# Fourier mixing followed by routed experts: x loaded in larger transfers, and the first stage of the third and fourth batch moved to other places in the head

## The chip, the cores and the metric

The kernel runs on one core of a Trainium2 chip. A core has TensorE (PE, matrix products; PEld in the profile is its loading of weights), VectorE (DVE), ScalarE (ACT), GpSimd (POOL) and SyncE (SP, which here only issues transfers). SP, ACT and POOL each have a queue of DMA transfers; 16 DMA engines move the data of all of them. The metric is the device time of one execution in microseconds (us). Durations in the profile come from one profiled execution.

## The reference

```python
X = np.fft.rfft(x, axis=1)                 # x: 8 batches x 2496 x 256, float32
Y = X * (filt_r + 1j * filt_i)[None]
y = np.fft.irfft(Y, n=2496, axis=1)        # then seen as 19968 rows of 256
expert_idx = token_ids * 2654435761 % 8
for e in range(8):
    h = np.maximum(y[expert_idx == e] @ w1[e], 0)    # w1[e]: 256 x 1024
    out[expert_idx == e] = h @ w2[e]                 # w2[e]: 1024 x 256
```

Each of the eight batches is filtered along its 2496 positions, and each resulting row then goes through the two layers of one of eight experts, chosen by its token's number.

## The kernel before

**Fourier part.** 2496 = 39 x 64. Positions of a batch are read as 39 x 64, and three of the 64 columns are put side by side, so that a product has 3 x 39 = 117 rows. A batch goes through four products. Stage 1 (`stage1`, tiles `pa`, line 267) transforms along 39 with the table `wf_t`; it is cut into six pieces `u`, two for each of three x parts `v`; the sixth piece is small (line 261). The forward product (`pb`, line 312) transforms along 64; VectorE multiplies with the filter (lines 318 and 322) and adds (line 323), which gives `y`. The back product (`pc`, lines 335 and 378) goes back along 64, and the inverse product (`pd`, line 267 in `stage3`) back along 39. Between stage 1 and the forward product, and between the back and the inverse product, rows and columns have to be exchanged. From the third batch on this goes through DRAM (`d1`, `d2`: written at lines 297, 342, 792 and 794, read by `load2`, line 303, into `low`, and by `load4`). For the first batch, and for the way back of the second, TensorE transposes (`pt` line 367, `pu` line 394). The results `o` are scattered to `xs` in DRAM, sorted by expert (line 433, on GpSimd's queue, four issues for a piece).

**Experts.** `xs` is cut into tiles of 256 rows. `step(i)` gathers a tile (`load`, `xg`, line 843), transposes it on VectorE (`xt`, line 854), forms sums of its halves (`st`, line 867) and of the weights (`tw`, line 876: GpSimd, for tile 0 VectorE), multiplies up (`up`, line 886, banks `up_a`, `up_b`, `up_c`), adds on VectorE (line 893), applies the ReLU on ACT (line 890), and multiplies down (`dps`, line 921). `ask` issues the gathers of a tile some steps ahead.

**Order.** Every engine has one program order. It comes from a list of pieces with due times. The head (`head`, lines 763 to 796) holds the first batch, the second, the third's stage 1 and four of six pieces of the fourth's stage 1, and ends with the gathers of tiles 0 and 1. All after it is `main`, whose pieces have due times in steps: `run_until` issues those that are due between the parts of an expert step. A piece's instructions go on all its engines at that place of the order, its transfers among them. The fourth batch is `batches[3]`, the third `batches[2]`; `first` and `second` are batches 0 and 1.

**Buffers.** The PSUM pool `fps` has four buffers in rotation, shared by `pa`, `pb`, `pc` and `pd`. `pa` is copied out by ACT. `high` holds the second batch's back products first, and then the fourth's stage 1 in two slots `t1`, so that the third x part's results go where the first part's were. x parts of the third and fourth batch use the pool `xpool` of two buffers. `put_off` collects writes to `d1` that are issued on SP after the first gathers. The loads of x (`load1`, line 249) are three transfers of 39 rows to a part, one for each third of the columns; one of the first batch's is on ACT's queue and all others are on SP's. Eight semaphores serve the transfers of SP and ACT in turn, so an issue waits for the transfer that used its semaphore last.

The numbers of lines are those of the kernel before; the changed kernel's are up to three higher behind line 290.

## Time and profile before

| | us |
|---|---|
| median of 6 runs | 1426.33 |
| lowest, highest | 1419.26, 1428.30 |
| profiled execution, whole | 1424.15 |
| its span in the profile | 1422.4 |
| TensorE busy in it | 1376.1 |
| last scatter of the second batch issued | 139.80 |
| first expert step's first product | 146.47 |
| second expert step's first product | 164.81 |

The span begins with the first instruction and ends with the last. A row of the timeline gives start, length, engine, line, operation, what it writes and reads, how many instructions stand together, and in brackets the idle time of the engine before it and who ended it. The chain of waits is followed back from the last instruction: each row's engine or transfer was what the next row waited for. The granted clock is the share of TensorE's full clock that it was given; over the whole span it was 0.988.

### The profile page before, as it was taken

The page shows a single profiled execution, that of the slowest core. Times are in us where ns is not written, and L with a number is a line of the kernel's source. Part 1 is how long each engine was busy: PE and PEld are TensorE (multiplying, and loading weights), DVE is VectorE, ACT ScalarE, POOL GpSimd, SP SyncE. Part 2 cuts the span into 40 slices and gives each one's busy share as a digit, 9 for nine tenths or more (in the row PEclk, how much of TensorE's full clock was granted, in tenths as well). Part 3 has the DMA queues.
Part 4 walks back from the last instruction along what each step waited for, and adds up shares of the span by engine and source line. Part 5 has one row for each costly group of instructions (what it writes and reads, how often), then busy time and mean ns, then how long its engine had stood idle before and what let it go on. Part 6 is the DMA issues. An engine that isn't in the chain of part 4 may idle for free.

```text
span 1422.4 us, 26307 instructions
## 1 busy us (share of the span) xinstructions
PE 1376.1 (97%) x9398; PEld 1276.4 (90%) x9398; DVE 888.2 (62%) x1630; ACT 417.3 (29%) x760; POOL 829.5 (58%) x735
## 2 busy tenths in 40 slices
PE   7989888999999999999999999999999999999997
PEld 7777777998888888889999899999999999999997
DVE  6673475575556466445666477656767776676775
ACT  3554122232223223232223222222222222222222
POOL 5166332854574565578533687788855566555563
PEclk8999999999999999999999999999999999999999
DMA  8685865767987598888754775887742526161611
GB/s 223 185 293 165 211 199 139 229 202 246 275 266 252 156 292 275 259 273 277 245 166 120 234 255 170 235 239 238 255 135 68 190 64 197 46 218 42 215 46 35
DMA packets 244650, 278.34 MB, mean 196 GB/s; under 512 B 125171, under 2 KB 213862, under 8 KB 235092
## 3 DMA queue, kind: packets, MB, share of 16 engines
q1 hardware_dynamic: 98020, 182.34, 40.9%
q10 hardware_dynamic: 126688, 50.07, 14.7%
q0 software_dynamic: 19808, 44.20, 8.8%
q8 instruction: 77, 1.26, 0.4%
q14 instruction: 57, 0.47, 0.1%
HBM read 293.65 MB, written 86.15 MB: 267 GB/s over the span
## 4 chain that ended last, share of the span: by engine, by line
PE 85%; DMA 8%; DVE 4%; issue 1%; ACT 1%; SPq 1%; ACTq 0%; POOLq 0%; POOL 0%; DVEq 0%
PE dps L921 20%; PE up_b L886 8%; PE up_a L886 5%; PE up_c L886 5%; PE pd L267 5%; PE pb L312 4%; PE dnc L948 4%; PE pa L267 4%; PE dnb L948 4%; PE dna L948 4%; PE upc L943 4%; PE upa L943 4%; PE pc L335 3%; DMA t<-d 2%; PE upe L943 2%; PE upb L943 2%
## 5 line engine op out<-in xcount | busy, mean ns | idle before, releaser
L921 PE MATMUL dps<-wts,ht 128*128 128x256 f32 x1600 | 367.0, 380 | 4.3 <-ACT ht L890 4.3
L921 PEld LDWEIGHTS dps<-wts,ht 128*128 128x128 f32 x1600 | 302.1, 190 | 47.7 <-ACT ht L890 5.5
L1013 POOL DMA_INDIRECT out_dram<-osb,no x158 | 164.4, 1040 | 222.8 <-DVE osb L955 137.3
L433 POOL DMA_INDIRECT xs<-o,sidx x176 | 178.4, 1014 | 167.4 <-ACT o L269 95.7
L876 POOL TENSOR_TENSOR tw<-wts 128x512 f32<-128x512 f32 x158 | 205.1, 1298 | 113.0 <-DMA wts<-in_moe_w_dram 88.7
L876 POOL TENSOR_TENSOR tw<-wts,tw 128x512 f32<-128x512 f32 x158 | 206.7, 1308 | 6.2
L893 DVE TENSOR_TENSOR ht<-up_b,ht 128x512 f32<-128x512 f32 x150 | 103.7, 692 | 113.6 <-PE up_b L886 91.3
L890 ACT ACTIVATE ht<-ht 128x512 f32<-128x512 f32 x150 | 94.3, 630 | 188.2 <-DVE ht L893 172.5
L322 DVE TENSOR_TENSOR z<-pb,filt 64x512 f32<-64x512 f32 x160 | 110.1, 688 | 30.8 <-PE pc L335 28.8
L926 DVE COPY osb<-dps 128x512 f32<-128x512 f32 x50 | 34.6, 691 | 148.1 <-PE dps L921 147.7
L886 PE MATMUL up_a<-xt,wts 128*128 128x128 f32 x800 | 115.7, 278 | 6.4 <-DVE xt L854 4.0
L886 PEld LDWEIGHTS up_a<-xt,wts 128*128 128x128 f32 x800 | 106.3, 194 | 10.0 <-DVE xt L854 4.4
L886 PE MATMUL up_b<-st,tw 128*128 128x128 f32 x800 | 107.4, 278 | 2.7 <-DVE ht L893 1.9
L886 PEld LDWEIGHTS up_b<-st,tw 128*128 128x128 f32 x800 | 98.2, 193 | 4.6 <-issue 4.6
L893 DVE TENSOR_TENSOR ht<-up_c,ht 128x512 f32<-128x512 f32 x100 | 69.1, 691 | 38.1 <-PE up_c L886 33.4
L952 ACT ACTIVATE ht<-ht 128x512 f32<-128x512 f32 x90 | 56.5, 630 | 122.5 <-DVE ht L955 76.6
L267 PE MATMUL pd<-t,wi_t 120*117 120x256 f32 x320 | 79.7, 393 | 2.9 <-DMA t<-d 2.3
L318 DVE TENSOR_TENSOR y<-pb,filt 128x512 f32<-128x512 f32 x80 | 55.2, 690 | 42.8 <-PE pb L312 40.6
L269 ACT COPY o<-pd 117x512 f32<-117x512 f32 x80 | 45.0, 585 | 102.1 <-PE pd L267 46.7
L267 PEld LDWEIGHTS pd<-t,wi_t 120*117 120x117 f32 x320 | 59.2, 189 | 15.6 <-DMA t<-d 3.0
L323 DVE TENSOR_TENSOR y<-y,z 128x512 f32<-128x512 f32 x80 | 71.1, 889 | 2.7
L312 PE MATMUL pb<-low,d_t 128*128 128x256 f32 x280 | 72.2, 381 | 0.0
(215 smaller groups left out, 2407.7 us busy)
## 6 DMA issues: line engine op xcount, KB each, us to landing
wts<-in_moe_w_dram SPq DMA_DIRECT2D x162, 1024.0 KB
xg<-xs ACTq DMA_DIRECT2D x321, 64.0 KB
low<-d SPq DMA_DIRECT2D x70, 256.0 KB
d_t<-t2s SPq DMA_DIRECT2D x15, 1024.0 KB
e_t<-t2s SPq DMA_DIRECT2D x15, 1024.0 KB
x<-in_x_dram SPq DMA_DIRECT2D x39, 312.0 KB
t<-d SPq DMA_DIRECT2D x12, 960.0 KB
raw<-in_moe_w_dram SPq DMA_DIRECT2D x8, 1024.0 KB
```

The source lines that it names most:

```text
L267: nc.tensor.matmul(out=ps[0:cols * H, k, :], lhsT=w[:], rhs=src[:, 2 * i + k, :], start=True, stop=True)
L312: nc.tensor.matmul(out=ps[:, i, :], lhsT=d_t[:, s, :], rhs=rhs, start=True, stop=True)
L322: nc.vector.tensor_tensor(out=z[b], in0=ps[a], in1=f_t[1][64 * hi:64 * hi + 64, s1:s1 + 2, :], op=OP.mult)
L433: st = nc.gpsimd.indirect_dma_start(out=xs[:], out_offset=bass.IndirectOffsetOnAxis(ap=index, axis=0), in_=rows, in_offset=None, bounds_ch ...
L876: eng.tensor_tensor(t[k][:], p, q, op=OP.subtract)
L886: nc.tensor.matmul(out=ps[bank][:, f, :], lhsT=w[:, f * P:(f + 1) * P], rhs=xx, start=first and f == 0, stop=True, skip_group_check=True)
L890: nc.scalar.activation(out=out, in_=in_, func=AF.Relu)
L893: nc.vector.tensor_tensor(out, ps[bank][:], other, op=OP.add)
L921: nc.tensor.matmul(out=ps[:, h, :], lhsT=ht[:, h, fp, :], rhs=w2[:, fp, :], start=(fp == 0), stop=(fp == FP - 1))
L943: nc.tensor.matmul(out=ps[:, f, :], lhsT=w[:, f * P:(f + 1) * P], rhs=xx, start=first and f == 0, stop=True, skip_group_check=True)
L948: nc.tensor.matmul(out=ps[:, 0, :], lhsT=a[:, f, :], rhs=b[:, f, :], start=first and f == 0, stop=True, skip_group_check=True)
L1013: st = nc.gpsimd.indirect_dma_start(out=out[:], out_offset=bass.IndirectOffsetOnAxis(ap=to_rows[i][:, h:h + 1], axis=0), in_=o[:, h, :], i ...
```

## The change

1. x is loaded in one transfer to a part, of 117 rows, all on SP's queue; the first part of the first batch in two transfers of four columns each. For this the rows of x and of the table `wf` stand in another order.
2. The third's stage 1 has other due times: its pieces 0 and 1 come before the second's last two back products, its piece 5 before the second's last inverse products, and no longer behind all of them.
3. All six pieces of the fourth's stage 1 are in the head, behind the second's inverse products. VectorE copies them out, not ACT. The write of x part 0's results to `d1` is issued at once on SP; those of parts 1 and 2 are put off. The last x part is loaded between pieces 1 and 2, into the buffer of the first.
4. In steps 0 and 1 the gathers of a later tile are asked for behind `up` and not inside it.

```diff
-        wf[:, h, h] = w
+        wf[:, H0[h] // HN, h] = w
...
-            for h in range(H):
-
-                (nc.scalar if self.b == 0 and h == 1 else nc.sync).dma_start(out=xt[h:NR:H, 0:n, :],
-                                  in_=bass.AP(tensor=x.tensor, offset=x.offset + (self.b * S + H0[h] + XL * v) * C,
-                                              ap=[[N2 * C, N1], [C, n], [1, C]]))
+            for j in (range(0, n, XG) if self.b == 0 and v == 0 else (0,)):
+                m = XG if self.b == 0 and v == 0 else n
+                nc.sync.dma_start(out=xt[:, j:j + m, :],
+                                  in_=bass.AP(tensor=x.tensor, offset=x.offset + (self.b * S + XL * v + j) * C,
+                                              ap=[[N2 * C, N1], [HN * C, H], [1, m * C]]))
...
-            self.products(wf_t, (NR, NR), 2 * NS, self.x[v][:, sl, :], self.t1[:, sl, :], nc.scalar.copy, u, "pa")
+            self.products(wf_t, (NR, NR), 2 * NS, self.x[v][:, sl, :], self.t1[:, sl, :],
+                          nc.vector.tensor_copy if self.b == 3 else nc.scalar.copy, u, "pa")
...
-                if (self.b == 2 and v > 0) or (self.b == 3 and v < 2):
+                if (self.b == 2 or self.b == 3) and v > 0:
...
-                    (nc.sync if self.b == 1 else nc.scalar).dma_start(out=dram, in_=chip)
+                    (nc.sync if self.b in (1, 3) else nc.scalar).dma_start(out=dram, in_=chip)
...
-    head += [(93.3 + 4.6 * u + 4 * (u > 3), lambda u=u: third.stage1(u)) for u in range(NU)]
+    head += [(t, lambda u=u: third.stage1(u)) for u, t in enumerate((87, 89.9, 93, 97.5, 107, 107.1))]
...
-    head += [(t, lambda v=v: fourth.load1(v)) for v, t in enumerate((110.5, 110.6))]
+    head += [(t, lambda v=v: fourth.load1(v)) for v, t in enumerate((95, 99, 118.025))]
...
-    head += [(123 + .1 * u, lambda u=u: fourth.stage1(u)) for u in range(4)]
+    head += [(t, lambda u=u: fourth.stage1(u)) for u, t in enumerate((118.01, 118.02, 118.03, 118.04, 118.1, 118.2))]
...
-    todo += part3(2, spaced(4.6, 7.5, NU), [4.0, 4.1, 4.8]) + part1(3, [None] * 4 + [1.5, 2], [None, None, .5])
+    todo += part3(2, spaced(4.6, 7.5, NU), [4.0, 4.1, 4.8])
...
-        up(i, ht, lambda: ask(i))
+        up(i, ht, (lambda: ask(i)) if i > 1 else (lambda: None))
+        if i < 2:
+            ask(i)
```

## The prediction

> **What bounds the kernel now.** I read the page first, then the windows of 10 us, then the chain of waits over the first 220 us, then the order in time around the gaps, and SyncE's queue.

> ```profile
> span 1422.4 us, 26307 instructions
> ...
> PE 1376.1 (97%) x9398; PEld 1276.4 (90%) x9398; DVE 888.2 (62%) x1630; ACT 417.3 (29%) x760; POOL 829.5 (58%) x735
> ...
> PEclk8999999999999999999999999999999999999999
> ```

> TensorE is busy for 97% of the span, so only its idle or half-clocked time can be won, and all but a few us of that lies before 200 us: after that a stage costs what its products cost, and a lead or a lag gained before it stays to the end. The digits of PEclk are all 9 but the first; two of the windows say where the rest of the clock goes (columns: stretch, length, busy us of PE, PEld, DVE, ACT, POOL, granted clock, DMA share, GB/s).

> ```profile
> 100.00:110.00 10.00, 6.22 (x29) 4.88 (x28) 5.59 (x9) 1.54 (x3) 1.86 (x2) 0.73 0.79 279
> ...
> 140.00:150.00 10.00, 6.04 (x28) 5.34 (x27) 2.48 (x5) 2.89 (x5) 5.67 (x5) 0.78 0.62 125
> ```

> TensorE is idle for 3.8 and 4.0 us there and the granted clock is 0.73 and 0.78. The chain of waits names what is behind it (start, us, what):

> ```profile
> 3.94 10.49 DMA wts<-in_x_dram
> ...
> 14.53 8.04 PE pa L357 x56
> ...
> 27.67 2.92 DVE y L323
> ...
> 34.42 2.78 PE pa L267 x8
> ...
> 108.95 3.23 PE pd L267 x8
> ...
> 139.80 2.31 DMA xs<-o,sidx
> ...
> 143.28 2.20 DMA xg<-xs
> ```

> Four places can be seen. x's second part lands at 14.43. A VectorE addition of 0.69 us takes 2.92 at 27.67, beside GpSimd's additions. A last inverse product of batch 1 takes 3.23 us (1.73 elsewhere) because the clock is down. The last scatter is issued at 139.80, after which the first gather goes out. The order in time shows the holes themselves (in brackets: idle before, and who ended it):

> ```profile
> 101.55 1.13 PE L378 MATMUL pc<-e_t,y 128*128 128x128 f32 x8 [1.25 <-DVE y L323]
> ...
> 104.40 1.79 PE L378 MATMUL pc<-e_t,y 128*128 128x128 f32 x8 [1.72 <-DVE y L323]
> ...
> 131.47 0.67 DVE L876 TENSOR_TENSOR tw<-wts 128x512 f32<-128x512 f32 x1
> ...
> 146.47 2.07 PE L886 MATMUL up_a<-xt,wts 128*128 128x128 f32 x8 [3.96 <-DVE xt L854]
> ```

> ```profile
> 157.80 7.17 PE L921 MATMUL dps<-wts,ht 128*128 128x256 f32 x32 [1.97 <-ACT ht L890]
> ...
> 180.79 1.96 PE L267 MATMUL pa<-x,wf_t 117*120 117x256 f32 x8 [2.65 <-DVE y L323]
> ```

> TensorE waits for VectorE before both last back products (1.25, 1.72), 3.96 before the first expert step, 1.97 before the first down product (ACT issued gathers from 148.79 to 156.58 and its ReLU came after them), and 2.65 before a product of the fourth batch that needs a PSUM buffer VectorE still reads.

> ```profile
> 42.43 18.98 SPq L297 DMA_DIRECT2D d<-high  x4
> 65.06 12.14 SPq L303 DMA_DIRECT2D low<-d  x10
> ...
> 146.23 3.25 SPq L792 DMA_DIRECT2D d<-low  x3
> 156.43 7.57 SPq L303 DMA_DIRECT2D low<-d  x8
> ```

> These four price a write to d and a load behind it: the write issued at 61.02 (640 KB) had landed when line 303 went on at 65.06, 4.0 us; the 1600 KB issued from 146.23 had landed at 156.43, 10.2 us, some gathers ahead of them in the queue.

> **The change, part by part.** Negative is a gain; times are those of the profiled execution (span 1422.4, 1424.15 whole), and 1424.15 is 2.2 under the median of 1426.33.

> A. Head loads. Nine x issues of batch 0 become four, all on SP; ACT's three go. Bytes are the same. SP's queue now brings x part by part: the 234 KB of part 2, most of which ACT's queue brought before part 1 was complete (14.43), come after it. By the 233 GB/s of 10 to 20 us that is 1.0 us; part 1's products start near 13.4. Stage 1 then ends 1 to 2 us earlier than 22.57. What is late next: batch 1's first x, in place near 30.4 (SP's issue at 30.42 waited for it); its products run at 34.42 now, so no more than 3.8 can be won before that. The addition at 27.67 may slip in ahead of GpSimd's (2.9 to 0.7) or not, if both move together. Bounds 0 and -3.8; I take -2.4, half way between 1.0 and 3.8, as I cannot tell which of the two the addition follows. SP's later x loads (one issue for three, 0.75 us each) and their bytes are as before, off the path: cost 0, bounds +1 and -1; SP is idle most of the time and the same bytes lie ahead of each weights load. The rows of a host table are permuted to match; its products are the same, cost 0.

> [...]

> B. Third's stage 1 earlier. Two of its pieces (3.46 us of products) fill the gap at 98.6 to 104.4. The second piece needs the PSUM buffer of the last forward product, read until 103.53, so: 103.6, two products of 0.87, then the last back product 0.89, done at 106.2, as now (104.40 + 1.79). ACT issues a write to d first (0.36), so the transposes start 0.3 later, but with the clock up they take 0.87 for 1.96 and the inverse product 1.73 for 3.23: first scatter near 110.6 for 111.98. From there to the end of batch 1's inverse products TensorE has 9.64 (pd) + 6.18 (pa) + 3.93 (pu) us, and five times about 0.5 of waiting for VectorE, as pa no longer stands between pu and pd: 130.8, now 132.5. The 22 scatters at 1.29 end at 139. Worth -1.7 to what follows, counted in C.

> C. Fourth's stage 1 whole. In TensorE's order: pieces 0 to 3 (6.9 us) from 130.8 to 137.7, then 4 and 5, then the first expert step. Its last x part reuses the buffer of the first: SP issues it after pieces 0 and 1 (134.2) and behind a write to d of 960 KB that waits for VectorE's copies (135.2). Both stand on SP ahead of the seven gathers. Both together are 1662 KB. By the two prices above, 4.0 us and 1022 KB more at 6.2 us per 960, that is 10.6, gathers included; by the best rate of the windows (316 GB/s from 80 to 90 us) and the 2.20 us of a gather's landing, 7.5. So x is there between 142.7 and 145.8; I take 144.0, nearer the middle than the upper end, which counts gathers that come behind here. Pieces 4 and 5: 2.7 us at full clock, 5.4 at half (3.23 for 1.73 above is nearly that); TensorE has been idle for 6 us, more than before 104.40, so I take 4.0. Then, in VectorE's queue, in this order: the last copies (0.9), four sums of weights (2.7, the 131.47 row: hidden at 131 to 134 now, with no cover then), the transposition (0.7). The first expert step starts at 152.3 for 146.47: +5.8; bounds +3.2 and +9.0. GpSimd's order does not change, and its own sums of weights come before VectorE's four. VectorE's copy costs 0.65 for ACT's 0.59 and delays nothing else; late gathers are no longer what it waits for.

> [...]

> D. The gathers of steps 0 and 1 are asked for after the step's ReLUs. First expert step to first down product: 157.80 - 146.47 = 11.33 now; 1.97 of it is the wait, and the products are 6.25 at full clock (164.97 to 171.24 in the next step). With no wait and one to three us lost to the clock: 8.3, so -3.0; bounds -2.0 and -5.0. Later by that: the gathers for step 2, wanted at 172 and in place by some 166; SP's last four line 303 loads, which wait on the same semaphores and are wanted in step 2. Cover enough.

> E. Steps 1 and 2 lose fourth's pieces 4 and 5: 1.73 + 0.99 of products, and the 2.65 of waiting, as a down product needing no such buffer follows instead. -5.4 at most, -2.7 at least if VectorE, which is nearly full from 172 to 182, makes TensorE wait a little later; I take -5.0, since the next product that wants VectorE's result (184.31) has it at 177.9.

> Sum: -2.4 + 5.8 - 3.0 - 5.0 = -4.6: 1424.15 - 4.6 = 1419.55, and on the median 1421.7.

> **Rivals.** (1) Slower: x's last part holds everything. The chain C is VectorE's queue behind one transfer, and each us of it is a us. With the gains at their lower bounds (A 0, D -2, E -2.7) it has to reach +9.0 to make +4.3: x at 147.2 in place of 144.0. For it: two transfers in one queue beside scatters; the DMA share was 0.92 from 120 to 130 us, when x came beside them. Against it: the 4.0 and 10.2 above. With x at 149.0: -4.7 + 10.8 = +6.1, 1432.4. (2) No difference: A is the bytes' order alone (-1.0), E only the removed products (-2.7), C +5.8, D -3.0: -0.9, 1425.4. For it: DMA share 0.94 to 0.99 from 10 to 40 us; against it: nothing but x waits there. (3) A larger gain: the addition escapes GpSimd (-3.8) and the clock stays up in C (+4.5) and D (-5.0), with E at -5.4: -9.7, 1416.6. For it: TensorE's gaps at 101 to 104 are filled; against it: the new gap before piece 4. (4) The change does not do what it says: the halves of x part 0 land, but TensorE's warm-up products run until 6.84 and part 1 decides; then A's halves are worth 0 and the rest stands (it is in the sum so).

> **How the numbers follow.** A measurement here tells about 0.3%, 4.3 us, from no change. My case, -2 to -8 (1418 to 1424), gets 0.45; as its middle lies just past -4.3, 0.27 of it is faster and 0.18 the same. (3) has 0.26, all faster; (2) 0.16, all the same; (1) 0.13, all slower; (4) is part of each. So faster 0.53, same 0.34, slower 0.13. All terms at their lower ends make -3.8 + 3.2 - 5.0 - 5.4 = -11.0, 1415.3, at their upper ends 0 + 9.0 - 2.0 - 2.7 = +4.3, 1430.6. The range goes 3 us below the first, as the runs shown spread from 1419.26 to 1428.30 and a median of a few moves with them, and leaves out the upper edge and most of (1): 1412 to 1430.

> **What would show it.** Right: part 1's stage 1 starts near 13.4; granted clock near 1 from 100 to 110; the last scatter issued near 138.5; pieces 4 and 5 of the fourth batch right after its last x, near 144 to 148, then four sums on VectorE, first expert step near 152 (A 2 us less on all of these); no wait of ACT's between the first up and down products; step 1 shorter by about 4.6, step 2 by 1. Wrong: a first expert step past 155, or steps 1 and 2 as long as now, or a step after 210 us that has changed its length.

## The result, and the profile after

The changed kernel is slower: median 1434.36 us (1430.21 to 1445.33, 20 runs) against 1424.79 us for the kernel before (1417.65 to 1439.13, 46 runs), ratio 1.0074, 95% interval 1.0058 to 1.009. Forecast were 1421.7 us and a range of 1412 to 1430. The profiled execution took 1435.17 us, span 1433.5, so it is 0.8 us over the median.

The page of the changed kernel (busy time by engine, and the granted clock in 40 slices):

```profile
span 1433.5 us, 26231 instructions
...
PE 1379.6 (96%) x9398; PEld 1278.2 (89%) x9398; DVE 895.9 (62%) x1642; ACT 410.9 (29%) x748; POOL 828.3 (58%) x735
...
PEclk9899899999999999999999999999999999999999
```

TensorE is busy for 96% where it was 97%: 3.5 us more of busy time, 11 us more of span. So most of the loss is idle time. The windows of 10 us (length, busy us of PE, PEld, DVE, ACT, POOL, granted clock, DMA share, GB/s) say where:

```profile
100.00:110.00 10.00, 8.17 (x49) 6.95 (x49) 5.59 (x10) 4.27 (x8) 1.97 (x2) 1.00 1.04 336
...
140.00:150.00 10.00, 2.20 (x5) 1.76 (x6) 0.13 (x1) 0.00 (x0) 2.24 (x2) 0.67 0.62 155
...
190.00:200.00 10.00, 7.14 (x45) 6.40 (x45) 8.59 (x13) 1.35 (x3) 4.06 (x4) 0.90 0.47 170
```

From 100 to 110 us the clock is 1.00, as forecast (0.73 before). From 140 to 150 us TensorE works for 2.20 us, for 6.04 before, and the clock is 0.67. The chain of waits (start, us, what) names the cause:

```profile
115.78 2.67 DMA xs<-o,sidx
...
136.95 10.71 DMA x<-in_x_dram
...
147.80 3.74 PE pa L267 x8
151.54 1.87 PE pa L261 x4
...
154.81 0.79 DVE tw L877 x2
...
157.38 2.07 PE up_a L887 x8
...
165.35 6.91 PE dps L922 x32
```

The transfer of the fourth batch's last x part, issued at 136.95, holds the end of the chain for 10.71 us; then its products, VectorE's sums of weights, and the first expert step at 157.38, which was 146.47 before. The order in time on TensorE (in brackets: idle before, and who ended it):

```profile
147.80 3.74 PE L267 MATMUL pa<-x,wf_t 117*120 117x256 f32 x8 [8.67 <-DMA x<-in_x_dram]
...
157.38 2.07 PE L887 MATMUL up_a<-xt,wts 128*128 128x128 f32 x8 [3.99 <-DVE xt L855]
...
165.19 7.07 PE L922 MATMUL dps<-wts,ht 128*128 128x256 f32 x32
...
188.46 1.10 PE L336 MATMUL pc<-y,e_t 128*128 128x256 f32 x4 [1.31 <-DVE y L324]
...
198.45 2.05 PE L887 MATMUL up_b<-st,tw 128*128 128x128 f32 x8 [2.78 <-DVE ht L894]
```

8.67 us of waiting for x, then pieces 4 and 5 in 5.6 us (147.80 to the end of the last product near 153.4) with the clock at one half, then 3.99 of waiting for VectorE. The wait for ScalarE ahead of the first down product (1.97 before) is gone. Further on there are two longer waits for VectorE, 1.31 (none there before) and 2.78 (0.91 before). SyncE's queue and GpSimd show what else stood behind that transfer:

```profile
136.47 0.38 SPq L298 DMA_DIRECT2D d<-high  x1
136.95 0.84 SPq L249 DMA_DIRECT2D x<-in_x_dram  x1
147.74 4.67 SPq L844 DMA_DIRECT2D xg<-xs  x7
```

```profile
137.77 0.90 POOL L434 DMA_INDIRECT xs<-o,sidx  x1 [0.30 <-issue]
147.68 1.26 POOL L877 TENSOR_TENSOR tw<-wts 128x512 f32<-128x512 f32 x1 [9.01 <-DMA x<-in_x_dram]
...
178.81 1.28 POOL L877 TENSOR_TENSOR tw<-wts 128x512 f32<-128x512 f32 x1 [26.08 <-DMA d<-high]
...
186.45 1.30 POOL L877 TENSOR_TENSOR tw<-wts 128x512 f32<-128x512 f32 x1
```

The write to d and the load of x go out at 136.47 and 136.95, the gathers only at 147.74: the last scatters, issued up to 137.77, were not complete before (by the trace's semaphore events the last one landed at 147.46, 9.7 us after its issue; before the change it took 2.31). GpSimd's sums start at 147.68, 0.22 us after that landing; the profile names x, which landed at 147.66, but in e6 below, where x is long there, the same sums start 0.22 us after the last scatter's landing too, so they wait for the scatters. VectorE in the same stretches:

```profile
153.43 0.74 DVE L264 COPY high<-pa 120x256 f32<-120x256 f32 x2 [1.17 <-PE pa L261]
...
156.62 0.70 DVE L855 STREAM_TRANSPOSE xt<-xg 128x512 f32<-128x512 f32 x1
...
180.28 1.31 DVE L868 TENSOR_TENSOR st<-st,xt 128x128 f32<-128x128 f32 x1
...
182.78 1.35 DVE L868 TENSOR_TENSOR st<-xt,st 128x128 f32<-128x128 f32 x1
...
186.17 2.14 DVE L324 TENSOR_TENSOR y<-y,z 128x512 f32<-128x512 f32 x1
```

The transposition that the first expert step needs (156.62) stands behind the last copies (153.43) and the four sums between them; the first gathers had landed by 151.8. In step 1 three small sums of tokens take 1.31 to 1.35 us each (0.28 alone) and an addition 2.14 (0.69 alone), while GpSimd's sums for steps 2 and 3 run (from 178.81 and 186.45).

Where the two profiled executions stand against each other (us from the start):

| mark | before | after | difference |
|---|---|---|---|
| first transposition of batch 0's inverse | 67.21 | 66.28 | -0.9 |
| last scatter issued | 139.80 | 137.77 | -2.0 |
| first expert step | 146.47 | 157.38 | +10.9 |
| first down product, step 0 | 157.80 | 165.19 | +7.4 |
| same, step 1 | 172.79 | 180.08 | +7.3 |
| same, step 2 | 199.05 | 205.66 | +6.6 |
| same, step 10 | 356.00 | 362.74 | +6.7 |
| same, step 34 | 796.87 | 808.94 | +12.1 |
| end | 1422.4 | 1433.5 | +11.1 |

The +5.4 between steps 10 and 34 is not the change's: that stretch took 440.9 us in the profiled execution of before, 446.2 in the changed kernel and 444.8 to 448.3 in the profiles of six other kernels from a chip on which the kernel before takes as long (e5 to e8, f5, f6), one of which (e8) differs from it only before step 2. The profile shown of before had a short stretch there. By the same kind of comparison its 11.33 us between first expert step and first down product was a long one (see D below). So the two profiles' difference of 11 us and the medians' of 9.6 agree, but not part by part.

### The profile page after: what moved, and what is told of

Its sections match the earlier page's. It is cut to its first block, busy times and chain, and to the rows that moved or that the text cites. A ratio compares the mean times of both kernels' runs of the same rounds, so it can differ in the third digit from the quotient of the medians.

```text
span 1433.5 us, 26231 instructions
## 1 busy us (share of the span) xinstructions
PE 1379.6 (96%) x9398; PEld 1278.2 (89%) x9398; DVE 895.9 (62%) x1642; ACT 410.9 (29%) x748; POOL 828.3 (58%) x735
## 3 DMA queue, kind: packets, MB, share of 16 engines
q8 instruction: 77, 1.26, 0.4%
## 4 chain that ended last, share of the span: by engine, by line
PE 85%; DMA 8%; DVE 4%; issue 1%; ACT 1%; ACTq 0%; SPq 0%; POOL 0%; POOLq 0%; DVEq 0%
PE dps L922 21%; PE up_b L887 9%; PE up_a L887 6%; PE up_c L887 5%; PE pd L267 5%; PE pb L313 4%; PE dnc L949 4%; PE dnb L949 4%; PE dna L949 4%; PE upc L944 4%; PE upa L944 4%; PE pa L267 4%; PE pc L336 3%; DMA xg<-xs 3%; DMA wts<-in_x_dram 2%; PE upe L944 2%
## 5 line engine op out<-in xcount | busy, mean ns | idle before, releaser
L323 DVE TENSOR_TENSOR z<-pb,filt 64x512 f32<-64x512 f32 x160 | 110.1, 688 | 26.2 <-PE pc L336 24.2
L927 DVE COPY osb<-dps 128x512 f32<-128x512 f32 x50 | 34.6, 691 | 145.9 <-PE dps L922 145.5
L894 DVE TENSOR_TENSOR ht<-up_c,ht 128x512 f32<-128x512 f32 x100 | 69.1, 691 | 38.2 <-PE up_c L887 33.4
L267 PE MATMUL pd<-t,wi_t 120*117 120x256 f32 x320 | 78.8, 390 | 4.7 <-DMA t<-d 2.5
L898 ACT COPY ht<-up_a 128x512 f32<-128x512 f32 x50 | 29.3, 587 | 170.4 <-PE up_a L887 133.8
```

Source lines behind the costliest of these rows:

```text
L267: nc.tensor.matmul(out=ps[0:cols * H, k, :], lhsT=w[:], rhs=src[:, 2 * i + k, :], start=True, stop=True)
L323: nc.vector.tensor_tensor(out=z[b], in0=ps[a], in1=f_t[1][64 * hi:64 * hi + 64, s1:s1 + 2, :], op=OP.mult)
L894: nc.vector.tensor_tensor(out, ps[bank][:], other, op=OP.add)
```

## The experiments

All ratios compare with the kernel before on the same chip. The chips are of two kinds here: on one the kernel before takes 1423 to 1426 us (also in the runs of the result), on two others 1463 to 1466. On the latter, engines stand idle in the head for 2 to 9 us at a time where the profile names nothing that they waited for, and the changed kernel itself is only 1.0026 and 1.0027. I couldn't find out why; marks are therefore compared as distances within one profile. The changed kernel was not run beside e5 to e8, f5 and f6; its 1.0074 is compared with theirs by way of the kernel before. A distance in one profile can also be off by several us: e1 and f4 are the same kernel, with 14.6 and 9.0 us in the fourth column.

| run | before on its chip | ratio (95%) | last scatter's issue to first expert step | from there to the first down product | to step 1's | to step 2's |
|---|---|---|---|---|---|---|
| before | 1425 | 1 | 6.7 | 11.3 | 15.0 | 26.3 |
| changed | 1425 | 1.0074 (1.0058 to 1.009) | 19.6 | 7.8 | 14.9 | 25.6 |
| e5 | 1426 | 1.0006 (0.9988 to 1.0023) | 16.1 | 6.4 | 16.2 | 23.4 |
| e6 | 1426 | 0.998 (0.9954 to 1.0005) | 11.2 | 8.0 | 14.9 | 20.5 |
| e7 | 1426 | 1.0024 (1.0002 to 1.0046) | 6.9 | 7.9 | 16.8 | 28.0 |
| e8 | 1426 | 0.9992 (0.997 to 1.0013) | 6.8 | 8.2 | 18.7 | 24.2 |
| f5 | 1423 | 0.9984 (0.9959 to 1.001) | 10.2 | 8.1 | 14.9 | 20.4 |
| f6 | 1423 | 1.0004 (0.9975 to 1.0034) | 7.0 | 7.9 | 19.5 | 23.9 |
| e1 | 1464 | 1.0012 (0.9979 to 1.0045) | 14.6 | 9.0 | 14.9 | 25.1 |
| e2 | 1464 | 1.0009 (0.998 to 1.0038) | 6.6 | 9.2 | 16.4 | 27.5 |
| e3 | 1464 | 1.0035 (1.0002 to 1.0068) | 27.0 | 8.0 | 14.9 | 22.4 |
| e4 | 1464 | 1.0021 (0.9982 to 1.006) | 14.0 | 8.9 | 14.9 | 22.9 |
| e9, changed | 1463 | 1.0026 (1.0 to 1.0053) | 19.3 | 8.1 | 14.9 | 24.7 |
| e10 | 1463 | 0.9951 (0.9927 to 0.9975) | 7.2 | 7.8 | 19.5 | 23.7 |
| e11 | 1463 | 0.9921 (0.9892 to 0.9949) | 11.8 | 7.8 | 14.9 | 21.2 |
| e12 | 1463 | 0.9946 (0.9917 to 0.9975) | 11.4 | 8.2 | 19.4 | 20.3 |
| f1, changed | 1466 | 1.0027 (0.9993 to 1.0061) | 18.2 | 8.7 | 14.9 | 25.3 |
| f2 | 1466 | 0.9939 (0.9911 to 0.9967) | 8.2 | 7.8 | 16.7 | 23.0 |
| f3 | 1466 | 0.9962 (0.9929 to 0.9995) | 6.8 | 8.0 | 19.8 | 23.6 |
| f4 | 1466 | 0.9973 (0.9942 to 1.0003) | 9.0 | 8.2 | 15.0 | 28.1 |

### What holds the first expert step

**e4: the last x part not loaded.**

```diff
-    head += [(t, lambda v=v: fourth.load1(v)) for v, t in enumerate((95, 99, 118.025))]
+    head += [(t, lambda v=v: fourth.load1(v)) for v, t in enumerate((95, 99))]
+    head += [(118.025, lambda: fourth.x.update({2: fourth.x[1]}))]
```

> The changed kernel without the transfer of the fourth batch's last x part (702 KB): its products read the second part in its place. Theory (that transfer holds pieces 4 and 5 and, in the same queues, the last scatters and so the gathers): the first expert step comes at 147 to 148.5 for 157.4, 9 to 10 us earlier, and the time is near the kernel before, ratio 1.000 to 1.002. Rival (the write to d of 960 KB ahead of it, or VectorE's copies and sums, hold the step): first expert step past 152, ratio over 1.004.

From the last scatter to the first expert step 14.0 us, where the changed kernel has 19.3 and 18.2 on such chips: 4 to 5 us shorter, not 9 to 10. Counted from the write to d, whose issue the same copies release, it is 15.1 (144.49 to 159.57) against 20.3 and 19.3. VectorE shows what was left:

```profile
151.35 1.29 DVE L269 COPY high<-pa 120x512 f32<-120x512 f32 x2 [3.47 <-DMA d<-high]
...
155.48 1.75 DVE L878 TENSOR_TENSOR tw<-wts 128x512 f32<-128x512 f32 x1
...
158.82 0.70 DVE L856 STREAM_TRANSPOSE xt<-xg 128x512 f32<-128x512 f32 x1
```

The copy of piece 4 waits 3.47 us for the write to d to land, whose buffer it takes; and the four sums that follow run beside GpSimd's sums and take up to 1.75 us in place of 0.69. So both sides were right by half: the x transfer is 4 to 5 us, the write to d and VectorE's queue the rest. The ratio, 1.0021, is just above the theory's range and under the rival's.

**e5: VectorE's sums moved into the wait for x.**

```diff
-    head += [(123.5, lambda: begin()), (123.6, lambda: [load(i) for i in range(2)])]
+    head += [(118.045, lambda: begin()), (123.6, lambda: [load(i) for i in range(2)])]
```

> The changed kernel with VectorE's four sums of weights for step 0 moved ahead of its copies of the fourth batch's pieces 4 and 5, into the wait for x. Theory (VectorE's queue is a part of the chain behind the last x): the first expert step comes 2.5 to 2.8 us sooner after piece 5's products than in the changed kernel (4.0 us of waiting there, 1.2 to 1.6 here), ratio 1.005 to 1.006. Rival (the gathers, issued behind the late scatters, hold the step as well): less than 1 us sooner, ratio 1.007.

```profile
151.44 3.74 PE L267 MATMUL pa<-x,wf_t 117*120 117x256 f32 x8 [8.28 <-DMA x<-in_x_dram]
...
157.81 1.16 PE L887 MATMUL up_a<-xt,wts 128*128 128x128 f32 x8 [1.46 <-DVE xt L855]
```

The wait before the first expert step is 1.46 for 3.99, 2.5 less, as the theory had it, and the gathers did not take over. The step itself stands at 157.81, no earlier than in the changed kernel (157.38), since the last scatter was issued 4.0 us later in this profile. The total gained more than the step, and more than the theory's 1.005 to 1.006: 1.0006 against 1.0074, whose intervals do not overlap. In the profile the shorter wait spares half-clock time too (6.4 us to the first down product for 7.8); from there step 1 is 1.3 us longer and step 2 2.2 shorter. From the last scatter to step 2's first down product that makes 6.0 us of the ratio's 9.7; the rest stays open.

**e6: the last x part in buffers of its own, loaded early, on top of e5** (the main lines).

```diff
+            if self.b == 3 and v == 2:
+                rest = ppool.tile([P, 2, C], F32, name="x_3_3", tag="p")
+                self.x[v] = [low[0:NR, 4, :].rearrange("p (j c) -> p j c", c=C), rest[0:NR]]
+                for j, m in ((0, XG), (XG, n - XG)):
+                    nc.sync.dma_start(out=self.x[v][j // XG],
+                                      in_=bass.AP(tensor=x.tensor, offset=x.offset + (self.b * S + XL * v + j) * C,
+                                                  ap=[[N2 * C, N1], [HN * C, H], [1, m * C]]))
+                return
...
-    head += [(t, lambda v=v: fourth.load1(v)) for v, t in enumerate((95, 99, 118.025))]
+    head += [(t, lambda v=v: fourth.load1(v)) for v, t in enumerate((95, 99, 99.5))]
```

> The kernel of e5 with the fourth batch's last x part in buffers of its own (a free slice of low and a free product buffer), loaded right behind its second part, at about 118 us, so that it's there before piece 4; the write to d stays. Theory: pieces 4 and 5 follow piece 3 without a gap; what remains is the write to d (960 KB), behind which the last scatters land 3 to 4 us late, so the first expert step comes 8.5 to 10 us after the last scatter's issue (6.7 in the kernel before, 19.6 in the changed kernel), 9 to 11 us sooner than in the changed kernel; steps 1 and 2 are 1 to 4 us shorter than before; ratio 0.997 to 1.000. Rival (the scatters, with more x beside them, are late by themselves): last scatter issued past 141, ratio over 1.003.

TensorE and GpSimd in that profile:

```profile
139.40 1.89 PE L277 MATMUL pa<-low,wf_t 117*120 117x256 f32 x8
...
149.35 2.07 PE L897 MATMUL up_a<-xt,wts 128*128 128x128 f32 x8 [7.08 <-DVE xt L865]
```

```profile
138.17 0.90 POOL L444 DMA_INDIRECT xs<-o,sidx  x1 [0.30 <-issue]
144.63 1.27 POOL L887 TENSOR_TENSOR tw<-wts 128x512 f32<-128x512 f32 x1 [5.57 <-DMA xs<-o,sidx]
```

Piece 4 follows piece 3 at once. The last scatter is issued at 138.17, and GpSimd goes on at 144.63: it landed at 144.41, behind the write to d (136.90 to 143.80). The first expert step comes 8.0 us sooner than in the changed kernel (9 to 11 expected; 11.2 after the scatter's issue, 8.5 to 10 expected), and step 1's down product to step 2's takes 20.5 us. Ratio 0.998, as expected; the rival (scatters late by themselves) is out.

**e11, f2, f5: also no write to d in the head.** The last part goes to a buffer of the inverse products, and all the writes are put off; e6's edit stays. The lines that this adds:

```diff
-            if half == 0:
+            if half == 0 and self.b == 3 and v == 2:
+                self.t1 = t4pool.tile([NK, XL, C], F32, name="t1_3_2", tag="t4")
+            elif half == 0:
...
-                if (self.b == 2 or self.b == 3) and v > 0:
+                if (self.b == 2 and v > 0) or self.b == 3:
```

> The kernel of e6 with the fourth batch's first write to d put off as well: its last part is copied to a free buffer of the inverse products (t4), so that no copy waits for that write. Theory (what was left in e6 is that write, behind which the last scatters landed at 144.4 for an issue at 138.2): the last scatter lands 2.2 us after its issue, the first expert step comes 6.5 to 7.2 us after it (11.2 in e6), 4 to 5 us earlier, ratio 0.994 to 0.996. Rival (the later writes to d hold the weights and the loads of steps 1 and 2 by as much): ratio 0.997 to 0.999.

> The kernel of e11 again. Theory: last scatter issued at 137.5 to 139, first expert step 6.2 to 7.2 us after it, at 144 to 146, 11 to 13 us before the changed kernel's; steps 1 and 2 shorter than before by 1 to 4 us; ratio to the kernel before 0.993 to 0.996. Rival (the gain of e11, 0.992, belongs to the chip on which the kernel before took 1463): 0.997 to 1.000.

> The kernel of e11 and f2 a third time. Theory: if the kernel before takes 1425 here, first expert step 6.2 to 7.2 us after the last scatter's issue, at 144 to 146, ratio 0.993 to 0.997; where it takes 1463, 0.992 to 0.995 as in e11 and f2. Rival: no gain where the kernel before takes 1425, ratio 0.998 to 1.001.

The last scatter lands 2.2 us after its issue in e11 and f5 (139.45, 141.66), 3.5 in f2: the write to d was the cause of its lateness. But the first expert step comes 10.2 us after the issue in f5 and 8.2 to 11.8 in the others, not 6.5 to 7.2. VectorE in f5:

```profile
141.47 0.68 DVE L889 TENSOR_TENSOR tw<-wts 128x512 f32<-128x512 f32 x1
...
145.41 1.75 DVE L889 TENSOR_TENSOR tw<-wts,tw 128x512 f32<-128x512 f32 x1
...
148.94 0.69 DVE L867 STREAM_TRANSPOSE xt<-xg 128x512 f32<-128x512 f32 x1
```

The gathers that the transposition needs had landed by 145.5; it runs at 148.94, behind sums that take up to 1.75 us beside GpSimd's and the copies. With the queue of DMAs cleared, VectorE's order holds the step. Ratios 0.9921, 0.9939 where the kernel before takes 1463 to 1466, 0.9984 where it takes 1423: it beats the changed kernel everywhere, the kernel before only where that takes 1463 to 1466. The changed kernel ran beside e11 and f2 on their chip (e9 and f1, 1.0026 and 1.0027), and the intervals are apart: with both transfers out of the way and the sums moved forward, what the change loses there is won back, and more. The next try would be the sums ahead of the fourth batch's copies altogether; it was not run.

### Asking late

**e8: asking late alone, on the kernel before.**

```diff
-        up(i, ht, lambda: ask(i))
+        up(i, ht, (lambda: ask(i)) if i > 1 else (lambda: None))
+        if i < 2:
+            ask(i)
```

> The kernel before with the gathers of steps 0 and 1 asked for after the ReLUs, nothing else. Theory (the 1.97 us wait before the first down product in the profile of before comes from slow issues beside the writes to d, and goes): first expert step to first down product 8.0 to 9.3 us for 11.33, ratio 0.998 to 0.999. Rival (in e1 and e3 the gathers asked for early were issued within 2.1 us and nothing waited, so the wait is not there in most executions): ratio 1.000, and a wait for ScalarE in step 1 in its place.

First expert step to first down product is 8.2 us for 11.3, as the theory had it, though e3 below shows that late asking isn't the reason. TensorE and ScalarE show the other side, which the rival named:

```profile
153.60 7.07 PE L921 MATMUL dps<-wts,ht 128*128 128x256 f32 x32
...
164.90 0.71 PE L886 MATMUL up_a<-xt,wts 128*128 128x128 f32 x4 [1.55 <-ACT ht L897]
```

```profile
160.24 3.30 ACTq L843 DMA_DIRECT2D xg<-xs  x4
163.57 0.59 ACTq L843 DMA_DIRECT2D no<-xs  x1
164.26 0.59 ACT L897 COPY ht<-up_a 128x512 f32<-128x512 f32 x1 [9.10 <-DMA xg<-xs]
```

The gathers that the first down product's spot asks for are issued until 164.2, and ScalarE's copy for step 1 stands behind them: TensorE waits 1.55 us, and a half-clock stretch (166.32 to 169.73) follows. Step 0's down product to step 1's takes 18.7 us for 15.0. In f6, f3 and e10, with the same asking, the wait is 2.68 to 3.18 us and the distance 19.5 to 19.8. So beside the profile shown of before 3.2 are won and 3.7 lost; ratio 0.9992. In the changed kernel, which asks late too, this loss is not there (14.9).

**e3: the changed kernel with asking as before** (the same three lines undone).

> The changed kernel with the gathers of steps 0 and 1 asked for ahead of the ReLUs, as before. Theory: asking late saves 3.5 us before the first down product, but GpSimd's sums for step 2 start 9 us later for it (178.8), fall on VectorE's work and cost 2 to 4 us in step 2; without it the first down product comes 11.3 us after the first expert step (7.8 now), the 2.8 us wait in step 2 goes, and the time is that of the changed kernel within 2 us: ratio 1.006 to 1.009. Rival (the prediction's step D alone): 3 to 3.5 us slower than the changed kernel, ratio 1.010.

Both missed. First expert step to first down product is 8.0 us although the gathers are asked for early: the wait isn't there. And step 2's wait of 2.78 is still there, so late asking doesn't cause it; GpSimd's sums for step 2 fell on VectorE's work here too. In e1 and f4, with early asking as well, the distance is 9.0 and 8.2. The 11.3 us of the profile shown of before is the only one of its kind among 20. (The 27.0 us from last scatter to first expert step in e3 are that execution's: the write to d was issued only 5 us after the last scatter, at 151.07. That scatter, with no write beside it, landed 2.2 us after its issue.)

### The head loads and the third's times

**e1, f4: the head loads alone; e7, e2: the changed kernel without the fourth batch's part; e10, f3, f6: these without the head loads; e12: e11 without the head loads.** Their edits are the change's own hunks, done alone or left out; e12 also loads the last x part by three transfers a piece.

> The kernel before with the head's x transfers alone changed. Theory: stage 1 of batch 0 ends 1.4 us earlier and TensorE is 1.0 us ahead at 60 us, as in the changed kernel; what is left of it behind the idle stretch near 62 to 72 us depends on how many half-clock windows follow, so the first expert step lies between 144.8 and 146.6 (146.47 before) and the time is 0 to 2 us under the kernel before, ratio 0.9985 to 1.000. Rival (the prediction's step A): the lead stays, 2.4 us at the first expert step and at the end, ratio 0.998.

> The kernel of e1 again: the head's x loads alone. Theory (a lead of 1.0 us at 60 us, which the clock takes back, and a last x part of the fourth batch that lands later in step 1, 8.8 us after its issue in one transfer): ratio 1.000 to 1.003. Rival (the prediction's step A): 0.998.

> The changed kernel with the fourth batch's stage 1 as before (four pieces in the head, two in the main part, copied by ScalarE): the head loads, the third's new times and the late asking stay. Theory: that part is the whole loss: last scatter near 138, first expert step near 144.5, 7.8 us from it to the first down product, so 5 to 6 us under the kernel before, 1419, ratio 0.996. Rival: asking late delays what SyncE's queue brings for steps 1 and 2 also here, and gives back 2 to 4 us there: ratio 0.998 to 1.000.

> The kernel of e2 again: head loads, third's times and late asking without the fourth batch's stage 1. Theory: 2 us from the scatters' earlier end, and the late asking worth 0 to 2 us: ratio 0.997 to 0.999. Rival: the late asking holds ScalarE's copies in step 1 (0.9 us of TensorE's time in e2) and gives all of it back: 1.000 or more.

> The kernel of e7 with the head's x loads as before: the third's new times and late asking alone. Theory (e7's loss of 0.2% against e8's -0.1% comes from the x loads in one transfer, which land later where a piece waits for them): last scatter 2 us earlier than in e8 relative to the second batch's last forward product, ratio 0.997 to 0.999. Rival (the third's new times cost it): ratio 1.001 to 1.003, as e7.

> The kernel of e10 again: the third's new times and late asking alone. Theory: as e10, 0.995 to 0.998. Rival (e7 with these and the head loads was 1.0024, so that the new times cost something where the kernel before takes 1425): 1.000 to 1.003.

> The kernel of e10 and f3 a third time. Theory (the head loads, not the third's times, made e7 slower than e8): where the kernel before takes 1425, 0.997 to 0.999; where it takes 1463, 0.995 to 0.997. Rival (the third's times cost): 1.001 to 1.003 where the kernel before takes 1425.

> The kernel of e11 with the x loads of the kernel before (three transfers for a part, batch 0's on two queues, none in halves). Theory (the head loads bring 1.0 to 1.9 us at 60 us and the idle stretch behind takes them back): within 1.5 us of e11, ratio within 0.001 of it. Rival (the head loads cost 2 to 4 us, as e7 against e8 suggests): ratio 0.0015 to 0.003 below e11's.

Against what was expected, only f3 lies in its theory's range. e7's ratio is its rival's; f4 came nearer its rival, and e1, e2, e10 and f6 fell outside both ranges. e12 lies 0.0025 above e11, where the rival had it below. The totals do not settle it: e1 1.0012 and f4 0.9973 are the same kernel, e12 is 0.9946 beside e11's 0.9921, with intervals that overlap; e7 at 1.0024 and f6 at 1.0004 differ by the head loads alone, also within their intervals, and e12 and e11 go the other way. e1's bounds for the first expert step missed (161.84) for the idle times of that chip. The marks say more. The first transposition of batch 0's inverse stands at 67.2, 64.7 and 65.8 us without the head loads (before, e8, f6; mean 65.9), and at 66.3, 69.5, 67.8, 67.2 and 66.8 with them (changed, e5, e6, e7, f5; mean 67.5); on the other chips at 62.9 to 63.7 without (e10, e12, f3), 63.7 to 67.3 with (nine profiles, mean 65.7). By these means the mark is 1.6 to 2.4 us later with the head loads, though the single profiles overlap. TensorE before, and then in the changed kernel:

```profile
14.53 8.04 PE L357 MATMUL pa<-wf_t,wts 117*128 117x120 f32 x56 [2.44 <-DMA wts<-in_x_dram]
...
30.64 2.08 PE L378 MATMUL pc<-e_t,y 128*128 128x128 f32 x8 [3.09 <-DVE y L323]
```

```profile
7.23 3.73 PE L358 MATMUL pa<-wf_t,wts 117*128 117x120 f32 x32
...
13.11 8.04 PE L358 MATMUL pa<-wf_t,wts 117*128 117x120 f32 x56 [1.79 <-DMA wts<-in_x_dram]
...
31.31 1.09 PE L267 MATMUL pa<-wts,wf_t 117*120 117x256 f32 x4 [2.26 <-DMA wts<-in_x_dram]
33.59 1.52 PE L267 MATMUL pa<-wts,wf_t 117*120 117x256 f32 x4 [1.18 <-ACT wts L381]
```

Part 0 lands in time for its products at 7.23, and they are over 0.7 us sooner than before; part 1 starts at 13.11 for 14.53. The idle time before it and a half-clock stretch behind it are there in both (2.44 us and 15.9 to 19.4 before, 1.79 and 13.7 to 17.1 now). The wait for the slow addition (3.09) is down to 0.89, and in its place TensorE waits for batch 1's first x (2.26) and then for a PSUM buffer that ScalarE reads (1.18). That x, in one transfer, has landed by 30.9 to 33.1 us in the five profiles with the head loads and by 30.4 to 31.0 in the three without. The two waits are 0.9 to 2.3 and 1.2 to 1.9 us in those five; of the three, e8 alone waits for that x (1.20). That they are what makes the later inverse is argued, not shown.

In step 1 the fourth's last x part, in one transfer, lands 8.8 us after its issue in e7, and its piece waits 1.75 us for it; in e1, e2 and f4 1.34, 2.39 and 2.95. The three transfers of e8 take 6.6 to 7.6 each and 9.1 from the first issue to the last landing, those of f6 7.1, and no such wait is there. So the single transfer is not shown to be slower; that a piece waits for it happens with three transfers too (2.65 us before).

The third's times did as forecast: from that first transposition to the last scatter's issue 72.6 and 73.9 us without them (before, e8), 69.1 to 72.8 with them (mean 71.5), 1.8 less, with ranges that overlap a little.

### The changed kernel again

> The changed kernel itself, on the chip of the runs beside it. Theory (one chip is like another): ratio 1.0058 to 1.009 as before, and so 6 to 8 us above e5, of which e5's 2.5 us in the wait explain a part only. Rival (the profile and the runs of the changed kernel came from a chip that suits it less): ratio 1.003 to 1.005.

> The changed kernel a third time, beside its parts on one chip. Theory: where the kernel before takes 1425, ratio 1.005 to 1.009 (1.0074 and 1.0026 so far, the second where the kernel before took 1463); its first expert step comes 10.5 to 11.5 us after the last x part is issued plus its 9.7 us of products, copies, sums and transposition, 19 to 20 us after the last scatter's issue.

1.0026 and 1.0027: neither range of e9's holds it, and e9's rival came nearer; f1's range was given for a chip on which the kernel before takes 1425, and this was not one. The long distance from last scatter to first expert step is there in both (19.3 us, and 18.2 where f1's text had 19 to 20), and the transfer of x takes 10.1 us in both. The kernel before has its own, larger idle times on those chips; where the rest of the ratio goes there stays open.

## Why the prediction was wrong

**What bounds the kernel** held: the loss and the gains all lie before 210 us, and the later steps keep what the head leaves them. Two lines were misread. The 2.65 us before the fourth's piece at 180.79 were put down to VectorE, as the profile does; but VectorE's last reading of PSUM ahead of it (line 322) ended at 179.98, and the addition named there reads none; the piece's x landed at 180.54, and in e1, e2 and e7 the profile names x. And the 1.97 us for ScalarE were read from one execution as a property of the order.

**A, head loads, -2.4.** Not there, and by the means above wrong in sign. Part 1 at 13.1 is within what was said (13.4), and the addition at 27.67 came down from 2.92 to 0.71, one of the two ways allowed for. That lead is 1.0 us at 58, and from 62 to 72 us it goes: in the changed kernel two stretches of half clock follow the same idle stretch, one in the kernel before. The windows of before and of after (columns as above):

```profile
63.72:67.14 3.42, 1.13 (x8) 0.97 (x8) 1.62 (x5) 0.93 (x2) 0.00 (x0) 1.00 0.33 93
67.14:70.55 3.41, 3.34 (x12) 2.75 (x13) 0.00 (x0) 1.19 (x3) 0.00 (x0) 0.50 0.90 302
70.55:73.96 3.41, 3.41 (x21) 2.99 (x20) 0.43 (x1) 2.15 (x4) 1.83 (x2) 1.00 0.83 298
```

```profile
61.48:64.89 3.41, 1.30 (x12) 1.14 (x12) 2.69 (x7) 0.69 (x1) 0.00 (x0) 1.00 0.48 132
64.89:68.31 3.42, 2.64 (x13) 2.07 (x12) 0.00 (x0) 1.31 (x3) 0.00 (x0) 0.50 0.72 213
68.31:71.72 3.41, 3.41 (x9) 2.44 (x10) 0.00 (x0) 1.14 (x2) 0.62 (x1) 0.50 0.88 306
```

In the changed kernel the second wait of that place (0.78 us) falls into the first half-clock stretch, and a second follows; before, both lie ahead of the stretch but for 0.07 us (the last section has the counts). Over eight profiles on one kind of chip the mark is 1.6 us later, not earlier. The bound of 0 left out the clock, and that batch 1's x, counted as landing where it did, comes later. One large transfer is not shown to bring its bytes sooner than three small ones: part 1 landed at 12.7 to 14.9 us in one transfer and 14.3 to 14.6 in three, batch 1's x not sooner.

**B, the third's stage 1, -1.7.** Right: 1.00 for 0.73, first scatter at 110.61 (110.6 said), last at 137.77 (138.5 to 139 said), 1.8 us over the profiles. Only batch 1's inverse products were through 1.2 us later than said (piece 0 of the fourth starts at 131.96, 130.8 said). In e5, e7 and f5 a half-clock stretch still fell on the first inverse product (3.5 to 3.6 us), so the clock is not safe there.

**C, the fourth's stage 1, +5.8.** This step failed, and it is the bulk of the loss: the first expert step comes at 157.38 and not at 152.3, +10.9 for a bound of +9.0. (A's lead is gone in this pair: the same inverse product of batch 0 starts at 73.33 and 73.44.) Two terms were too small. The first is the transfer of x: its products start at 147.80, not 144.0. Of these 3.8 us, 1.3 are the issue of the write to d ahead of it, at 136.47 and not at 135.2, since TensorE came to piece 0 1.2 us later than said and the write waits for VectorE's fourth copy (136.41); 2.4 are the write and load themselves, which took 11.2 us, 1662 KB (of 1024 bytes) at 152 GB/s, where 8.8 had been taken and 7.5 to 10.6 allowed. Why they run at no more than that is not shown. x landed at 147.66, past the 147.2 from which rival 1 was to decide. The second term is pieces 4 and 5, which ran at half clock throughout, 5.6 us for the 4.0 taken; the 5.4 named there for half clock, twice the 2.7 at full clock, was nearer. VectorE's queue after the copies, 4.3 us, was right (3.99 of waiting): 3.8 + 1.6 - 0.3 are the 5.1 missed. Not counted at all was that the two transfers hold back the last scatters, and with them the gathers: in e6, with x there early, the write alone kept the step at 11.2 us after the last scatter. That C is all of the loss is not shown: e7, without it, is still at 1.0024 (1.0002 to 1.0046).

**D, asking late, -3.0.** The number fits in that place (7.81 for 11.33), by luck, and the step is worth nothing: in e3, e1 and f4 the distance is 8.0 to 9.0 without it, and in e8 step 1 is 3.7 longer with it. The prediction asked what the later gathers hold up and looked at step 2's tokens and SyncE's loads; it did not look at ScalarE's own queue in step 1, which costs in e8, though not in the changed kernel (14.9 us there).

**E, steps 1 and 2 without pieces 4 and 5, -5.0.** The price was right within 1 us, and the changed kernel got 0.7 of it. From step 1's down product to step 2's it takes 25.6 us for 26.3; with GpSimd's sums clear of VectorE's work, in e6 and f5, 20.5 and 20.4, a gain of 5.8. In the changed kernel the stalls of VectorE in that stretch (time of the four sums of tokens and four additions beyond 0.28 and 0.69 each) come to 4.8 us, in e6 and f5 to 0.6 and 1.0, in the kernel before to 1.8. TensorE then waits 1.31 and 2.78, and a half-clock stretch follows at 198. The condition named for the lower bound, a VectorE that is nearly full, was the one that held; the bound of -2.7 did not allow for stalls.

**The rivals.** Rival 1 (x's last part holds everything) is what happened, by the mechanism named and past the point given; its 1432.4 us is 2 us short of the median. That its first expert step (157.3) agrees so well with 157.38 is in part luck: x came 1.3 us before the 149.0 it took, and pieces 4 and 5 took 1.6 longer. It had a chance of 0.13. Rival 3 counts C as +4.5 with a clock that stays up; no run shows that term: in the changed kernel pieces 4 and 5 took 5.6 us at a granted clock of 0.50, and the first expert step came 10.9 us later. Rival 4 (the halves worth nothing) holds for the halves.

Summed with the sizes from the runs: +10.9 (A, B and C up to the first expert step), D 0, E -0.7: +10.2, against +9.6 measured.

## What to carry to other kernels

Before work is moved into a gap, list what its transfers run beside, not only what stands behind them in the queue that issues them: here the last scatter, on GpSimd's queue, landed 9.7 us after its issue beside a write and a load on SyncE's, for 2.31 before and 2.2 without that write in e11 and f5, and everything that reads what the scatters wrote came later. A wait that the profile shows once is a price only if it is there in other executions. An operation that moves beside another engine's work may slow both (in f5 VectorE's sums of weights took up to 1.75 us for 0.68 and GpSimd's up to 1.71 for 1.26), so the gain depends on what runs beside what. And where a gap of about 2 us is left, as here, a half-clock stretch follows or not by where the gap falls (one step, two or none in the three profiles below), so a gain of 1 us ahead of such a gap can't be read from one profile.

## What the runs showed of the hardware

In f5 VectorE's sums of weights, whose two operands are outside PSUM, took 1.64 to 1.75 us for 0.68 while GpSimd's ran; its copies from PSUM right behind them, with GpSimd's last sum still on, took 1.27 us for two, where a single one takes 0.69 without it, so these were not slowed. GpSimd's own sums take longer too, 1.40 to 1.71 us in f5 for 1.26 in e6, where VectorE had done its own before.
